# Start addresses of the activation tiles between two chained matrix products

## The chip, the cores and the metric

The kernel runs on one core of a Trainium2 chip. The metric is the device time of one execution in microseconds; less is better. The figure for the kernel before is the median of three runs.

## The reference

Attention with a causal mask over 2 batches, 12 heads, 448 positions and a head width of 64 gives 896 tokens of 768 features. Two MLPs follow, one on the other's output, each with a hidden width of 2048:

```
attn = softmax(scale * q @ k.T, causal) @ v          # [2, 12, 448, 64]
x = attn.transpose(0, 2, 1, 3).reshape(896, 768)
h = np.maximum(x @ w_in, 0.0);  x = h * h @ w_out    # first MLP
h = x @ w_in;  out = (h - np.tanh(h)) @ w_out        # second MLP
```

All is float32. The MLPs are 4 products of 896 x 768 x 2048.

## The kernel before

**Pieces.** To keep float32 accuracy, every operand of the MLPs is held as a high and a low part of type fp32r, one tile with both. A product of two such operands is three matmuls (`pieces`, lines 426 to 428): high weights by high activations, high weights by low activations, low weights by high activations. The weights are the stationary operand (128 x 128, one weight load for each matmul), the activations the moving one (128 x 448: one batch of tokens).

**Stages.** After attention (with the first groups of the first MLP woven in) come four halves: two MLPs, each with its hidden width in two halves. A half has an h stage and an o stage, of 288 matmuls each. In the h stage, `first` runs 16 groups of 18 matmuls (6 blocks of x, for 8 hidden blocks m and 2 batches b), and `act1` or `act2` makes an activation of each result, whose two parts are written by `hi_of` (ScalarE, line 436) and `lo_of` (VectorE, line 439). In the o stage, `second` runs 12 groups of 24 matmuls (8 hidden blocks k, for 6 output blocks m and 2 batches b) over these activations. Its results are added to `part`, become the next MLP's input (the x tiles again, then named y), or are written out. The order of instructions on each engine is that of the code, written out by hand.

**Tiles.** The input lies in 6 tiles x0 to x5 (y for the second MLP). The weights lie in a ring of 8 tiles w, filled from raw by three VectorE and two ScalarE instructions for each unit (`w_prep`). The activations g lie in 8 slots. A slot's tile is [P, 2, 2, S]: high or low, two hidden blocks, 448 tokens. `gdst` gives hidden blocks 2j and 2j + 1 of batch b the slot (5, 6, 0, 1, 3, 2, 4, 7)[4 b + j]. So in an o group of batch 0 blocks 0 to 3 come from slots 5 and 6, and 4 to 7 from slots 0 and 1. In a group of batch 1 blocks 0, 1 come from slot 3, blocks 2, 3 from slot 2, blocks 4, 5 from slot 4, blocks 6, 7 from slot 7. The same slots serve attention first: slots 0 to 2 hold the probabilities p, 3 and 4 their transposes pt, 7 the last rows of v (vend).

**Addresses.** Tiles lie one after another in each partition in the order in which the code first names them. Start addresses in bytes, modulo 256, as the built program has them: x (and y) 160; the ring w 96; slots 0, 1, 2 and 7 at 192; slots 3 to 6 at 96. The sizes of x, w and g tiles, of one block of 448 values and of one 128-column block of weights are all multiples of 256 bytes. So every x lies 64 bytes above its weights modulo 256, every g of slots 3 to 6 lies 0 above, and every g of slots 0, 1, 2 and 7 lies 96 above. Modulo 1024, each of these classes takes several values: both operands change with batch, part and block.

Of the kernel before, what the change touches and what calls it, by code (L numbers as in the profile page):

```python
# [9 lines left out]
F32R = mybir.dt.float32r  # L10
# [9 lines left out]
B, H, S, D = 2, 12, 448, 64  # L20
DM = H * D
DFF = 2048
P = 128
# [4 lines left out]
NPAIR = B * NP  # L28
NQ = S // D
RING = 8  # L30
UNIT = 6
UC = UNIT * P
NU = 2 * (KF + DFF * DM // (P * UC))
# [50 lines left out]
def body(ctx: ExitStack, tc: tile.TileContext, qT, kT, vL, w1, w2, w3, w4, out):  # L84
# [9 lines left out]
    def slot(i, shape, dt, name):  # L94
        return sb.tile(shape, dt, tag=f"slot{i}", name=name)
# [72 lines left out]
    def ring(u):  # L168
        taken.append(u)
        return sb.tile([P, 2, UC], F32R, tag="w", bufs=RING, name=f"w{u}")  # L170

    def room():
        i = len(taken) - RING
        return i < 0 or taken[i] < freed[0]
# [85 lines left out]
    def hbank(name):  # L260
        n = hcount[0] % 8
        hcount[0] += 1
        tag, bufs = ("s", 4) if n < 4 else ("t", 2) if n < 6 else ("oh"[n - 6], 1)
        return ps.tile([P, 512], F32, tag=tag, bufs=bufs, name=name)[:, :S]
# [152 lines left out]
    g = {}  # L417
# [13 lines left out]
    def group(*args):  # L431
        for _ in pieces(*args):
            pass
# [58 lines left out]
    gt = {}  # L492

    def gdst(l, half, m, b):

        if m % 2 == 0:
            i = (5, 6, 0, 1, 3, 2, 4, 7)[4 * b + m // 2]
            gt[b, m // 2] = slot(i, [P, 2, 2, S], F32R, f"g{l}_{half}_{b}_{m // 2}")
        t = gt[b, m // 2]
        g[m, b] = (t[:, 0, m % 2], t[:, 1, m % 2])  # L500
        return g[m, b]
# [5 lines left out]
    def first(l, half, m, b):  # L507

        u = (2 * l + half) * 2 * HALF + m
        dst = gdst(l, half, m, b)  # L510
        h = hbank(f"h{u}_{b}")
        for _ in first_pieces(l, half, m, b, h):
            pass
        if b == 1:
            freed[0] = u + 1
        return lambda: (act1, act2)[l](h, dst)


    def early(count):
        for m in range(count):  # L520
            dst = gdst(0, 0, m, 0)
            h = ps.tile([P, 512], F32, tag="h", bufs=1, name=f"h{m}_0")[:, :S]
            for k, _ in enumerate(first_pieces(0, 0, m, 0, h)):
                if k == KD - 1:
                    done.append((h, dst))
                yield
# [28 lines left out]
    def second(l, half, m, b):  # L555
        u0 = (2 * l + half) * 2 * HALF + HALF
        o = hbank(f"o{u0}_{m}_{b}")
        group(o, lambda k: (u0 + (m * HALF + k) // UNIT, (m * HALF + k) % UNIT), HALF, lambda k: g[k, b])
        if b == 1:
            freed[0] = u0 + (m + 1) * HALF // UNIT  # L560
        if half == 0:
# [26 lines left out]
    for s in range(NPAIR + 2):  # L588
        p, a = s - 1, s - 2
        ss, sp, sa = s < NPAIR, 0 <= p < NPAIR, a >= 0  # L590
        f = s - 2 >= NP
# [158 lines left out]
```

## Time and profile before

| what | before |
|---|---|
| median of 3 runs | 546.22 us (546.01 to 546.26) |
| the profiled execution's own time | 546.67 us |
| its span, first to last instruction | 544.9 us |
| TensorE matmul busy / weight load busy | 538.6 us / 483.6 us |
| VectorE / ScalarE / GpSimd busy | 346.5 us / 327.7 us / 3.2 us |
| MLP matmuls in h stages / in o stages | 1152 / 1152 |

The four o stages start 132.88, 249.33, 365.78 and 482.23 us after the span's start, the h stages of the second to fourth half 191.72, 308.17 and 424.61 us after it. Busy time of matmuls is from issue to a modelled end, and overlaps the next one. How fast TensorE goes is read from the distance of one start to the next, called the pitch here.

### The profile page before, as it was taken

To read this page: it belongs to the slowest core of one execution; us is meant where nothing else is said; L and a number is where in the kernel's file an instruction comes from. 1 tells how busy PE (TensorE), PEld (TensorE's weight loads), DVE (VectorE), ACT (ScalarE), POOL (GpSimd) and SP (SyncE) were. 2 spreads that over 40 slices of the span, in tenths; PEclk is the share of its full clock that TensorE was granted. 3 is DMA by queue.
4 is the path that set the end of the run, shared out by engine and by line. 5 is a ranking of instruction groups with operands and counts; after the bars stand their busy time and mean duration, and the time that the engine had idled before them with its cause. 6 is when DMAs were issued, how large, how long until landed. Compare 5 with 4: busy or idle time off the path is not lost.

```text
span 544.9 us, 8255 instructions
## 1 busy us (share of the span) xinstructions
PE 538.6 (99%) x3206; PEld 483.6 (89%) x3206; DVE 346.5 (64%) x730; ACT 327.7 (60%) x630; POOL 3.2 (1%) x21
## 2 busy tenths in 40 slices
PE   8999999999999999999999999999999999999997
PEld 5777878899999999999999999999999999999996
DVE  5998997664525155543554688988653588887301
ACT  6999996677424276664332388876543688854100
POOL 1000000000000000000000000000000000000000
PEclk9999999999999999999999999999999999999999
DMA  8862323352524243331333230113655301026111
GB/s 297 282 202 64 114 89 98 112 187 99 184 109 140 92 124 109 115 117 58 117 115 117 64 112 0 59 58 119 228 179 170 117 1 58 1 75 220 39 52 51
DMA packets 16022, 61.86 MB, mean 114 GB/s; under 512 B 1712, under 2 KB 7344, under 8 KB 15984
## 3 DMA queue, kind: packets, MB, share of 16 engines
q1 hardware_dynamic: 15696, 61.00, 33.6%
q8 instruction: 25, 0.41, 0.3%
q10 hardware_dynamic: 288, 0.34, 0.2%
q14 instruction: 13, 0.11, 0.1%
HBM read 58.59 MB, written 2.75 MB: 113 GB/s over the span
## 4 chain that ended last, share of the span: by engine, by line
PE 94%; DVE 3%; ACT 2%; issue 0%; DVEq 0%; POOLq 0%; ACTq 0%
PE h L426 14%; PE o L428 14%; PE o L427 14%; PE o L426 14%; PE h L428 14%; PE h L427 14%; PE o L378 3%; PE s L298 2%; PE t L366 2%; DVE p L313 1%; ACT p L331 1%; ACT pt L373 1%; DVE p L352 1%; PE warm L244 1%; DVE x L414 0%
## 5 line engine op out<-in xcount | busy, mean ns | idle before, releaser
L428 PE MATMUL o<-g,w 128*128 128x448 f32 x384 | 140.9, 367 | 0.0
L427 PE MATMUL o<-g,w 128*128 128x448 f32 x384 | 140.7, 366 | 0.0
L426 PE MATMUL o<-g,w 128*128 128x448 f32 x384 | 140.6, 366 | 0.0
L427 PEld LDWEIGHTS o<-g,w 128*128 128x128 f32 x384 | 72.1, 188 | 6.4
L428 PEld LDWEIGHTS o<-g,w 128*128 128x128 f32 x384 | 72.1, 188 | 6.4
L426 PEld LDWEIGHTS o<-g,w 128*128 128x128 f32 x384 | 72.1, 188 | 6.2
L426 PE MATMUL h<-x,w 128*128 128x448 f32 x192 | 71.3, 371 | 0.0
L426 PE MATMUL h<-y,w 128*128 128x448 f32 x192 | 69.7, 363 | 0.0
L428 PE MATMUL h<-x,w 128*128 128x448 f32 x192 | 69.7, 363 | 0.0
L428 PE MATMUL h<-y,w 128*128 128x448 f32 x192 | 69.6, 362 | 0.0
L427 PE MATMUL h<-x,w 128*128 128x448 f32 x192 | 69.4, 362 | 0.0
L427 PE MATMUL h<-y,w 128*128 128x448 f32 x192 | 69.1, 360 | 0.0
L137 DVE SCALAR_TENSOR_TENSOR raw<-raw 128x768 int32<-128x768 int32 x64 | 61.0, 954 | 12.1 <-ACT raw L123 12.1
L140 ACT CAST w<-raw 128x768 fp32r<-128x768 f32 x56 | 50.3, 899 | 26.9 <-DVE raw L137 26.9
L123 ACT ACTIVATE raw<-raw 128x768 f32<-128x768 f32 x64 | 58.9, 920 | 0.1
L153 DVE TENSOR_TENSOR w<-raw,w 128x768 fp32r<-128x768 f32 x32 | 30.6, 958 | 34.9 <-ACT w L140 34.8
L566 ACT COPY part<-o 128x448 f32<-128x448 f32 x24 | 12.8, 534 | 57.9 <-PE o L428 57.9
L151 DVE SCALAR_TENSOR_TENSOR w<-w,raw 128x768 fp32r<-128x768 f32 x32 | 30.6, 957 | 24.3 <-ACT w L140 24.2
L439 DVE TENSOR_TENSOR g<-r,g 128x448 fp32r<-128x448 f32 x32 | 20.0, 624 | 41.0 <-ACT g L436 41.0
L331 ACT ACTIVATE p<-p,st 128x320 f32<-128x320 f32 (+6 forms) x84 | 41.0, 516 | 4.0 <-DVE st L313 3.9
L428 PEld LDWEIGHTS h<-y,w 128*128 128x128 f32 x192 | 36.0, 188 | 2.9
L428 PEld LDWEIGHTS h<-x,w 128*128 128x128 f32 x192 | 36.1, 188 | 2.5
(57 smaller groups left out, 726.1 us busy)
## 6 DMA issues: line engine op xcount, KB each, us to landing
raw<-w SPq DMA_DIRECT2D x64, 768.0 KB, 4.2
q<-qT SPq DMA_DIRECT2D x12, 224.0 KB, 5.4
k<-kT SPq DMA_DIRECT2D x11, 224.0 KB, 3.8
out<-part SPq DMA_DIRECT2D x11, 224.0 KB, 1.9
v<-vL SPq DMA_DIRECT2D x2, 576.0 KB, 7.4
v<-vL SPq DMA_DIRECT2D x1, 1152.0 KB, 6.0
k<-kT ACTq DMA_DIRECT2D x1, 224.0 KB, 3.5
vend<-vL SPq DMA_DIRECT2D x2, 96.0 KB, 7.3
```

Of the source, the lines that this page charges most:

```text
L123: nc.scalar.activation(h, h, AF.Prelu, scale=2.0**-112, alpha=2.0**32)
L137: nc.vector.scalar_tensor_tensor(out=lo, in0=hi, scalar=3, in1=lo, op0=ALU.logical_shift_left, op1=ALU.bitwise_or)
L140: act_late.append(lambda: nc.scalar.copy(out=st["w"][:, 0], in_=lo.bitcast(F32)))
L151: nc.vector.scalar_tensor_tensor(out=w[:, 1], in0=w[:, 0].bitcast(F32), scalar=-(1.0 - 2.0**-24), in1=f, op0=ALU.mult, op1=ALU.add)
L153: nc.vector.tensor_sub(out=w[:, 1], in0=f, in1=w[:, 0])
L331: nc.scalar.activation(p, p, AF.Exp, bias=st[:, 0, i : i + 1], scale=-1.0, **kw)
L378: return nc.tensor.matmul(ob[n][D * j : D * j + D, o], lhsT=vs[b][kc][rows, D * h : D * h + D], rhs=rhs, skip_group_check=True, **flags).ins
L426: nc.tensor.matmul(h, lhsT=hi, rhs=xh, start=(k == 0), stop=False)
L427: nc.tensor.matmul(h, lhsT=hi, rhs=xl, start=False, stop=False)
L428: nc.tensor.matmul(h, lhsT=lo, rhs=xh, start=False, stop=(k == kk - 1))
L439: nc.vector.tensor_sub(out=dst[1], in0=v, in1=dst[0])
L566: nc.scalar.copy(out=part[m][:, b], in_=o)
```

## The change

Each slot's tile becomes 64 floats (256 bytes) longer, and g is a view into it that starts 56 floats (224 bytes) into slots 0, 1, 2 and 7, and 16 floats (64 bytes) into slots 3 to 6. With 192 + 224 = 416 and 96 + 64 = 160, every g then starts at 160 modulo 256, as x does. The tiles p, pt and vend of attention still start at their slot's begin. A slot takes 256 bytes more, so all that lies behind it moves by a multiple of 256: w by 1536 bytes against x (six slots lie ahead of it), the slots by 0 to 1792.

```diff
+LINE = 64
+G_AT = (56, 56, 56, 16, 16, 16, 16, 56)
...
         if m % 2 == 0:
             i = (5, 6, 0, 1, 3, 2, 4, 7)[4 * b + m // 2]
-            gt[b, m // 2] = slot(i, [P, 2, 2, S], F32R, f"g{l}_{half}_{b}_{m // 2}")
+            n = 2 * 2 * S
+            t = slot(i, [P, n + LINE], F32R, f"g{l}_{half}_{b}_{m // 2}")
+            gt[b, m // 2] = t[:, G_AT[i] : G_AT[i] + n].rearrange("p (z k s) -> p z k s", z=2, k=2)
         t = gt[b, m // 2]
```

## Rows read from the trace of the kernel before

**Rows 1.** Page, parts 1 and 2: busy time; granted TensorE clock by slices, in tenths.
```profile
PE 538.6 (99%) x3206; PEld 483.6 (89%) x3206; DVE 346.5 (64%) x730; ACT 327.7 (60%) x630; POOL 3.2 (1%) x21
...
PEclk9999999999999999999999999999999999999999
```
**Rows 2.** Page, part 4: chain that ended last, by engine.
```profile
PE 94%; DVE 3%; ACT 2%; issue 0%; DVEq 0%; POOLq 0%; ACTq 0%
```
**Rows 3.** Weight loads by line: count, busy us, mean ns, idle us before them.
```profile
L427 PEld LDWEIGHTS o<-g,w 128*128 128x128 f32 x384 | 72.1, 188 | 6.4
L426 PEld LDWEIGHTS o<-g,w 128*128 128x128 f32 x384 | 72.1, 188 | 6.2
L428 PEld LDWEIGHTS o<-g,w 128*128 128x128 f32 x384 | 72.1, 188 | 6.4
...
L428 PEld LDWEIGHTS h<-y,w 128*128 128x128 f32 x192 | 36.0, 188 | 2.9
...
L426 PEld LDWEIGHTS h<-y,w 128*128 128x128 f32 x192 | 36.0, 188 | 1.9
...
L427 PEld LDWEIGHTS h<-y,w 128*128 128x128 f32 x192 | 35.9, 187 | 2.5
```
**Rows 4.** Timeline of TensorE, last half: start us, duration us; stages' ends.
```profile
424.61 0.36 PE L426 MATMUL h<-y,w 128*128 128x448 f32 x1
...
482.23 0.36 PE L426 MATMUL o<-g,w 128*128 128x448 f32 x1
...
540.86 0.37 PE L428 MATMUL o<-g,w 128*128 128x448 f32 x1
```
**Rows 5.** Timeline of TensorE: two o groups, each slot's first matmul.
```profile
487.12 0.36 PE L426 MATMUL o<-g,w 128*128 128x448 f32 x1
...
488.33 0.37 PE L426 MATMUL o<-g,w 128*128 128x448 f32 x1
...
489.57 0.37 PE L426 MATMUL o<-g,w 128*128 128x448 f32 x1
...
490.79 0.37 PE L426 MATMUL o<-g,w 128*128 128x448 f32 x1
...
492.03 0.37 PE L426 MATMUL o<-g,w 128*128 128x448 f32 x1
...
494.46 0.37 PE L426 MATMUL o<-g,w 128*128 128x448 f32 x1
...
496.93 0.36 PE L426 MATMUL o<-g,w 128*128 128x448 f32 x1
```
**Rows 6.** Windows, last h and o stage: length, busy by engine (count), clock, DMA.
```profile
424.60:482.10 57.50, 57.50 (x289) 53.88 (x288) 48.92 (x83) 46.72 (x83) 0.00 (x0) 1.00 0.16 55
482.20:541.20 59.00, 59.00 (x289) 53.89 (x288) 24.52 (x36) 12.88 (x17) 0.00 (x0) 1.00 0.24 83
```
**Rows 7.** Timeline, all engines, at the last o stage's beginning.
```profile
485.51 0.61 DVE L439 TENSOR_TENSOR g<-w,g 128x448 fp32r<-128x448 f32 x1
...
486.50 0.37 PE L426 MATMUL o<-g,w 128*128 128x448 f32 x1
...
490.32 0.96 DVE L153 TENSOR_TENSOR w<-raw,w 128x768 fp32r<-128x768 f32 x1 [0.49 <-ACT w L140]
```
**Rows 8.** Low parts, line 439: count, duration ns min, median, max.
```profile
L439 DVE TENSOR_TENSOR g<-w,g x32: 612/616/627, 319.9 to 487.3; 128x448 fp32r<-128x448 f32 x32
L439 DVE TENSOR_TENSOR y<-part,y x12: 617/619/627, 255.8 to 309.8; 128x448 fp32r<-128x448 f32 x12
```
**Rows 9.** Weight loads of attention that read slots, or whose matmuls do.
```profile
L366 PEld LDWEIGHTS t<-ident,p 128*128 128x128 f32 x168 | 18.9, 141 | 3.0 <-ACT pt L373 0.6 <-issue 0.4 <-DVE p L352 0.3
...
L378 PEld LDWEIGHTS o<-pt,v 128*64 128x64 f32 x144 | 9.4, 136 | 9.7 <-issue 3.5 <-ACT pt L373 3.3 <-DVE st L313 0.3
L378 PEld LDWEIGHTS o<-pt,v 64*64 64x64 f32 x144 | 6.2, 133 | 2.1 <-issue 1.2 <-ACT p L331 0.3 <-ACT r L547 0.3
L378 PEld LDWEIGHTS o<-pt,vend 64*64 64x64 f32 x48 | 3.7, 132 | 0.4 <-POOL token L402 0.4
```

## The prediction

> **What bounds the kernel now.** I read the page first. [...] The chain of waits lies on PE for 94% [rows 2], so a nanosecond taken off a matmul counts unless a wait fills it. A busy share of 99% does not say that the matmuls go as fast as they can, since their ends are modelled and overlap. So I went on to the weight loads by line, where idle time between loads shows [rows 3], then to the starts in the timeline [rows 4 and 5], then to a table of two stages [rows 6], and last to the producers with least time in hand [rows 7].
>
> The weight loads are all 188 ns long, but those of o stages have more idle time before them. The o rows sum to 3 x 72.1 busy and 6.4 + 6.2 + 6.4 idle, 235.3 us for 1152, or 204.3 ns each. The h rows with y sum to 107.9 + 7.3 = 115.2 us for 576, or 200.0 ns each [rows 3]. The starts say the same: 424.61 to 482.23 us is 288 pitches of 200.1 ns (taken within each stage of the last three halves, unrounded, 200.04), and 482.23 to 540.86 us is 287 pitches of 204.3 ns [rows 4]. All four o stages have 204.3.
>
> The instructions of both are the same in shape. Is it then the operands' addresses? Within an o stage the pitch goes by the slot that is read. In the group of batch 1 from 487.12, slots 3 and 4 take 1.21 and 1.22 us for 6 matmuls, slots 2 and 7 take 1.24 and 1.24. In the group of batch 0 from 492.03, slots 5 and 6 take 2.43 us for 12 matmuls (202.5 ns), slots 0 and 1 take 2.47 (205.8) [rows 5]. These are two of 48 groups. Over all 48, from the same timeline, slots 5 and 6 have 203.0, slots 3 and 4 202.9, slots 0 and 1 205.4, slots 2 and 7 205.8. So g that stands 0 above its weights modulo 256 costs 203, g that stands 96 above costs 205.6, and x, 64 above, costs 200.0. The same two slot classes recur in both batches at other places of the group, so the place in the group doesn't make it. Nor does other engines' traffic: the last h stage, with VectorE busy 48.92 us and ScalarE 46.72, is the faster one; the last o stage has 24.52 and 12.88 [rows 6].
>
> **The change part by part.** No instruction is added or removed, no queue's order changes, no wait is added.
>
> *The o matmuls.* Every g comes to x's residue, 160, while w stays at 96. The pairs then stand 64 apart, and x's pairs take all four values that this allows modulo 1024 and run at one pitch. I take x's pitch: 1152 x (204.29 - 200.04) = 4.90 us less. Bounds: nothing, if addresses don't act; as the most, the smallest pitch that recurs in the trace, 197 to 198 ns (one of three matmuls in every h block, followed by two of 201), 1152 x 7 = 8 us; that one is part of a triple whose mean is 200, so I keep 200.0.
>
> *Writers and readers of g.* ScalarE's and VectorE's writes start at another offset. Low parts written to y, whose tiles have the new residue already, take 619 ns at the median, to g 616 [rows 8]: 3 ns longer each, under 0.1 us for 16 in an h stage, on an engine that isn't the bound there. I cost it at nothing; a longer write would first show where the least time is in hand (below).
>
> *Attention.* p, pt, vend and one v tile move by multiples of 256, so their residues modulo 256 stay. Whether a longer period counts there no row shows. The loads concerned sum to 38.2 busy and 15.2 idle, 53.4 us [rows 9]. If they changed by what separates the two slot classes, 2.6 of 204 ns or 1.3%, that is 0.7 us either way. I take 0.
>
> *The h stages.* x's residues and w's stay modulo 256: 0. w moves 1536 bytes against x; that is a rival below.
>
> *What is late next.* A faster o stage brings each use nearer to its producer. The tightest is the last g of batch 0 in the second MLP: its low part ends 485.51 + 0.61 = 486.12, and its first matmul, the 22nd of the o stage, starts 486.50 [rows 7]. 0.38 us in hand; 21 x 4.25 ns take 0.09 of it and leave 0.29. Next is a weight unit: VectorE ends 491.28 [rows 7], the matmul starts 494.46 [rows 5], 60 matmuls into the stage, so 3.18 goes to 2.92. These producers start from the h results before them, so gains of earlier stages move both sides alike. Nothing stalls. Behind the last matmul, 540.86, stands a tail of some 4 us to the span's end that the change doesn't touch.
>
> *The sum.* 546.67 (the profiled execution) - 4.90 = 541.77. That execution lies 0.45 us above the median, 546.22, so for a median: 546.22 - 4.90 = 541.3 us, 0.9% less.
>
> [...] The rows above show the pitch going with the slot, 203 to 205.6, at the same weights [rows 5]. [...]
>
> **The rivals.**
>
> 1. *Only part of it is the distance.* Modulo 64 a distance of 64 is the same as 0, which slots 3 to 6 have already. If that were the rule, those 576 matmuls would gain nothing, the other 576 would fall from 205.6 to 203.0, 1.5 us: 544.7. For it: the two classes within o are the only contrast with all else equal; h differs from o also in group length and in the tiles its weights come from. Against it: the 200 of h would then need another cause, and the o pitch within slots 3 to 6 swings between 202 and 207 by block, which no x block does. Chance 0.09.
>
> 2. *Addresses don't act; the pitch goes by something that the slot number stands for*, such as the order of the blocks in the group. Then 0: 546.2. Against it: the classes recur at other places in batch 0 and batch 1. Chance 0.07.
>
> 3. *A longer period counts, and the ring's move spoils the h stages.* w goes 1536 bytes away from x. If the quiet pairing of x rested on a period above 1024, the h stages could take the o pitch, 1152 x 4.25 = 4.9 us more, and o, paired after another distance than x was, would gain nothing: 551.1. If only h lost it and o won it the two would cancel; so it decides the sign from the point where h loses more than o gains. Against it: x tiles lie 7168 bytes apart and ring tiles 6144, so pairs in h already stand at many distances, and every x block has one pitch. Chance 0.05.
>
> **How the numbers follow.** The forecast has 0.79, and its own range is 540.6 to 542.1: 0.7 us of attention either way, and the spread of medians. The range for 8 in 10 reaches to 540.2 at the low end (a part of the low bound) and to 543.4 at the high end, for a partial gain between forecast and first rival. About 0.2%, 1.1 us, is what a measurement of this kernel can tell from no change. Faster by more than that: 0.79 and most of the first rival, 0.07, is 0.86. Same: the second rival and the rest of the first, 0.09. Slower: the third, 0.05.
>
> **What would show it.** Right: idle time before o loads falls from 19.0 us to about 14.6; the o pitch is 200 in every slot, so an o stage takes 57.4 us from first to last start instead of 58.6, and the three later ones start about 1.2, 2.4 and 3.7 us earlier; h rows stay at 200.0; no idle at the 22nd matmul of an o stage. Wrong: slots 3 to 6 stay at 203 (first rival), all o pitches stay (second), h pitch rises above 200 (third), or transposes and value products change their pitch, which would show attention's bound to count.

## The result, and the profile after

The changed kernel takes 541.26 us (median of 4 runs, 540.96 to 541.73), the kernel before beside it 546.24 us (546.01 to 546.61): ratio 0.9908, 95% interval 0.9896 to 0.9920. The forecast was 541.3 us, range 540.2 to 543.4.

The profiled execution of the changed kernel took 541.23 us, its span 539.4 us. Lines 31 to 497 of the code have moved by two, so 426 to 428 are now 428 to 430. The weight loads by line (count, busy us, mean ns, idle us before), against [rows 3]:

```profile
L428 PEld LDWEIGHTS o<-g,w 128*128 128x128 f32 x384 | 72.1, 188 | 5.6
L429 PEld LDWEIGHTS o<-g,w 128*128 128x128 f32 x384 | 72.1, 188 | 3.7
L430 PEld LDWEIGHTS o<-g,w 128*128 128x128 f32 x384 | 71.8, 187 | 5.1
...
L428 PEld LDWEIGHTS h<-y,w 128*128 128x128 f32 x192 | 36.0, 188 | 2.7
L429 PEld LDWEIGHTS h<-y,w 128*128 128x128 f32 x192 | 36.0, 188 | 2.0
...
L430 PEld LDWEIGHTS h<-y,w 128*128 128x128 f32 x192 | 35.9, 187 | 2.6
```

The loads are as long as before. The idle time before o loads is 14.4 us in place of 19.0 (14.6 was forecast); h is as it was. In the timeline of TensorE (start us, duration us), the last half's stage ends, against [rows 4]:

```profile
420.46 0.36 PE L428 MATMUL h<-y,w 128*128 128x448 f32 x1
...
478.06 0.36 PE L428 MATMUL o<-g,w 128*128 128x448 f32 x1
...
535.46 0.36 PE L430 MATMUL o<-g,w 128*128 128x448 f32 x1
```

h: 57.60 us over 288 pitches, 200.0 ns. o: 57.40 over 287, 200.0 ns, where it was 204.3. From these and the rows of before, the saving at successive places is 4.15 us at the last h stage's start, 4.17 at the last o stage's, 5.40 at the last matmul. Three o stages lie ahead of the first two places and the fourth behind them, so the last o stage brings 1.23, and four of them 4.9. Another 0.4 us is there before the first o stage begins (132.46 us against 132.88). Nothing ties that part to the change: in the ten experiments below whose x and w keep their distance, this start lies anywhere from 132.12 to 132.90 us. The medians, 4.98 us apart, hold the o stages' 4.9 and next to nothing else.

By slot, against [rows 5], the first o groups of batch 1 and batch 0 in the last stage:

```profile
482.86 0.36 PE L428 MATMUL o<-g,w 128*128 128x448 f32 x1
...
484.06 0.36 PE L428 MATMUL o<-g,w 128*128 128x448 f32 x1
...
485.26 0.36 PE L428 MATMUL o<-g,w 128*128 128x448 f32 x1
...
486.46 0.36 PE L428 MATMUL o<-g,w 128*128 128x448 f32 x1
...
487.66 0.36 PE L428 MATMUL o<-g,w 128*128 128x448 f32 x1
...
490.06 0.36 PE L428 MATMUL o<-g,w 128*128 128x448 f32 x1
...
492.46 0.36 PE L428 MATMUL o<-g,w 128*128 128x448 f32 x1
```

1.20 us for 6 matmuls and 2.40 for 12, in every slot. The producers with least time in hand, against [rows 7], in the timeline of all engines:

```profile
481.34 0.61 DVE L441 TENSOR_TENSOR g<-w,g 128x448 fp32r<-128x448 f32 x1
...
482.26 0.36 PE L428 MATMUL o<-g,w 128*128 128x448 f32 x1
...
486.18 0.96 DVE L155 TENSOR_TENSOR w<-raw,w 128x768 fp32r<-128x768 f32 x1 [0.51 <-ACT w L142]
```

The last g ends at 481.95 and is used at 482.26: 0.31 us in hand (0.29 forecast). The weight unit ends at 487.14 and is used at 490.06 (the row above): 2.92, as forecast.

### The profile page after: what moved, and what is told of

The parts are those of the page before. It is cut to its first block, busy times and chain, and to the rows that moved or that the text cites. A ratio compares the mean times of both kernels' runs of the same rounds, so it can differ in the third digit from the quotient of the medians.

```text
span 539.4 us, 8255 instructions
## 1 busy us (share of the span) xinstructions
PE 532.9 (99%) x3206; PEld 482.7 (89%) x3206; DVE 346.2 (64%) x730; ACT 327.5 (61%) x630; POOL 3.2 (1%) x21
## 4 chain that ended last, share of the span: by engine, by line
PE 93%; ACT 3%; DVE 3%; DMA 1%; issue 0%; DVEq 0%; POOLq 0%; ACTq 0%
PE h L428 15%; PE o L429 14%; PE h L429 14%; PE o L428 14%; PE h L430 14%; PE o L430 14%; PE o L380 3%; PE s L300 2%; PE t L368 2%; ACT p L333 2%; DVE p L315 1%; ACT pt L375 1%; DVE p L354 1%; DMA k<-kT 1%; DVE x L416 0%; DVE w L155 0%
## 5 line engine op out<-in xcount | busy, mean ns | idle before, releaser
L429 PE MATMUL o<-g,w 128*128 128x448 f32 x384 | 139.4, 363 | 0.0
L428 PE MATMUL o<-g,w 128*128 128x448 f32 x384 | 139.2, 362 | 0.0
L430 PE MATMUL o<-g,w 128*128 128x448 f32 x384 | 138.2, 360 | 0.0
L134 DVE TENSOR_SCALAR raw<-raw 128x768 int32<-128x768 int32 x64 | 35.5, 555 | 7.1 <-DMA raw<-w 7.1
```

The lines of the kernel that those rows point to most:

```text
L134: nc.vector.tensor_scalar(out=lo, in0=lo, scalar1=29, scalar2=None, op0=ALU.logical_shift_right)
L428: nc.tensor.matmul(h, lhsT=hi, rhs=xh, start=(k == 0), stop=False)
L429: nc.tensor.matmul(h, lhsT=hi, rhs=xl, start=False, stop=False)
L430: nc.tensor.matmul(h, lhsT=lo, rhs=xh, start=False, stop=(k == kk - 1))
```

## The experiments

A pitch below is the mean time from one matmul's start to the next in one trace, over a whole stage or over a slot's 24 blocks of six matmuls. Where one stage holds one distance for 288 matmuls, its slots agree within half a ns (at distance 56 within 0.8). "Distance" is start of g (or x) less start of w, in bytes modulo 256. "Against" sets a time beside that of the kernel before, measured alongside.

**1. Only the room.**

```diff
-G_AT = (56, 56, 56, 16, 16, 16, 16, 56)
+G_AT = (0, 0, 0, 0, 0, 0, 0, 0)
```

> The slots keep their 256 extra bytes, but every g starts at its slot's begin again. Distance theory (the start distance of g to its weights modulo 256 sets the pitch, 64 giving 200 ns): distances 0 and 96 return, o pitch 204.3 ns, 546.2 us, the gain is gone whole. Rival, the room: the longer slots, which move the weight ring by 1536 bytes and the slots by 256 to 1792, make the gain; then the o pitch stays 200.0 and the time 541.3 us.

Measured 545.96 us against 546.37, ratio 0.9997 (0.9988 to 1.0006). The idle before o loads is back:

```profile
L429 PEld LDWEIGHTS o<-g,w 128*128 128x128 f32 x384 | 72.1, 188 | 6.5
L428 PEld LDWEIGHTS o<-g,w 128*128 128x128 f32 x384 | 72.1, 188 | 6.3
L430 PEld LDWEIGHTS o<-g,w 128*128 128x128 f32 x384 | 72.1, 188 | 6.4
```

19.2 us against 19.0 before. The o pitch is 204.3 and h stays at 200.04, though the ring and the slots have moved by their multiples of 256. So the start of g inside its slot makes the whole gain, and the rival of the room falls.

**2. Offsets for four slots.**

```diff
-G_AT = (56, 56, 56, 16, 16, 16, 16, 56)
+G_AT = (56, 56, 56, 0, 0, 0, 0, 56)
```

> Only slots 0, 1, 2 and 7 get their offset (distance 64); slots 3 to 6 stay at distance 0. Distance theory: slots 0, 1, 2, 7 at 200.0 ns, slots 3 to 6 at about 203.0, o mean 201.5; 576 x 3.0 ns = 1.7 us above the changed kernel, 543.0 us. Rival, uniformity: what counts is that all pairs have one and the same distance, so that a mix of two costs in every slot; then slots 0, 1, 2, 7 stay above 202 ns too and the time is 544.5 us or more.

Measured 545.06 us against 546.37, ratio 0.9976 (0.9966 to 0.9985): 2 us more than the distance theory said. The timeline of TensorE, a group of batch 1 and one of batch 0:

```profile
486.01 0.37 PE L428 MATMUL o<-g,w 128*128 128x448 f32 x1
...
487.25 0.36 PE L428 MATMUL o<-g,w 128*128 128x448 f32 x1
...
488.45 0.37 PE L428 MATMUL o<-g,w 128*128 128x448 f32 x1
...
490.89 0.37 PE L428 MATMUL o<-g,w 128*128 128x448 f32 x1
...
493.37 0.36 PE L428 MATMUL o<-g,w 128*128 128x448 f32 x1
...
495.77 0.37 PE L428 MATMUL o<-g,w 128*128 128x448 f32 x1
```

Slot 2 (distance 64) takes 1.20 us for 6, and slots 0 and 1 take 2.40 for 12: 200 ns, beside neighbours of another distance. Uniformity falls. But slot 3 takes 1.24, and slots 5 and 6 take 2.48 for 12: 206.7 ns at distance 0, where the same slots had 203 in the kernel before and in experiment 1. Only their neighbours' distance had changed, from 96 to 64. A matmul's pitch is not set by its own distance alone. Nor is it only the matmuls next to a change of distance that differ: slot 6, the seventh to twelfth matmul in a row at distance 0, has 202.3 on average in the kernel before and 206.7 here.

**3 and 4. A distance of its own for each slot**, in steps of 32 bytes, and the steps between.

```diff
-G_AT = (56, 56, 56, 16, 16, 16, 16, 56)
+G_AT = (40, 48, 56, 24, 32, 40, 48, 32)    # 3
+G_AT = (44, 52, 60, 28, 36, 44, 52, 36)    # 4
```

> Each slot gets a distance of its own to the weights modulo 256: slots 0 to 7 at 0, 32, 64, 96, 128, 160, 192, 224 bytes. Distance theory: slot 0, formerly 96 and now 0, goes to about 203 ns; slot 2 (64) has 200.0; slot 3, formerly 0 and now 96, goes to about 205.6; h stages stay at 200.0; the others show the curve, expected between 200 and 208. Rival, the slot's place (its number, or its place in the group): the pitch stays with the slot, slots 0 and 3 do not swap their classes. Rival, uniformity: all eight slots at 203 or more.

> The same at the distances between: slots 0 to 7 at 16, 48, 80, 112, 144, 176, 208, 240 bytes. Distance theory: a smooth curve between the values of the even map, with a flat stretch of 200 ns near 64 if 64 is no isolated point. A distance below 200.0 ns anywhere would point to a faster version. Rival, the slot's place: the same slots as in the other map are slow, whatever their distance.

Pitches of slots 0 to 7: 205.1, 204.5, 200.3, 205.2, 201.8, 206.2, 202.2, 204.5 in the even map; 202.0, 202.8, 203.2, 204.0, 205.0, 204.2, 203.8, 202.4 in the odd one (one trace each; 545.76 and 545.49 us). Slot 2, now at 64 by itself, is within 0.3 ns of the 200.0 of x (205.8 before), so the rival of the slot's place falls. Slots 0 and 3 did not swap 205.6 for 203 as the distance theory expected; both stand at 205. In slot 0 at distance 16 the six pitches of a block average 205, 207, 200, 200, 200, 200: the pitch changes within a block, and these maps mix the distance with what came before.

**5, 6 and 7. One distance for all slots.**

```diff
-G_AT = (56, 56, 56, 16, 16, 16, 16, 56)
+G_AT = (40, 40, 40, 0, 0, 0, 0, 40)      # 5: distance 0
+G_AT = (0, 0, 0, 24, 24, 24, 24, 0)      # 6: 96
+G_AT = (8, 8, 8, 32, 32, 32, 32, 8)      # 7: 128
```

> Every g at distance 0 from its weights modulo 256. Theory of the prediction (a matmul's pitch goes by its own distance alone: 0 gives 203, 96 gives 205.6, 64 gives 200): o pitch 203.0 ns, 541.3 + 1152 x 3.0 ns = 544.7 us. Theory of the carried state (after the run with four offsets, where slots 3 to 6 ran at 206.8 ns beside neighbours at 64, but at 203 beside neighbours at 96): the pitch also goes by the distance of the matmuls before, and with one distance throughout it settles at 206.8 ns, with one and the same triple of pitches in every block; 541.3 + 1152 x 6.8 ns = 549.1 us. Theory of uniformity (any single distance does): 200 ns, 541.3 us.

> Every g at distance 96. Own distance alone: o pitch 205.6 ns, 547.7 us. Carried state: a settled value between 200 and 209 ns, the same triple in every block, not tied to 205.6; 541.3 to 551.7 us. Uniformity: 200 ns, 541.3 us.

> Every g at distance 128, half of the period. Own distance alone: the 201.8 ns that slot 4 had at 128 in the even map, 543.3 us. Carried state: a settled triple, any value from 200 ns up. If 200.0 ns is a floor that other things set, nothing lies below it; a pitch under 200 would make a faster kernel than the changed one.

Measured 549.02 us against 546.18 (ratio 1.0051, 1.0035 to 1.0068) at 0, 547.25 (1.0023, 1.0013 to 1.0032) at 96, 545.73 in one run at 128. The weight loads of o, in this order of kernels:

```profile
L429 PEld LDWEIGHTS o<-g,w 128*128 128x128 f32 x384 | 72.1, 188 | 7.2
L428 PEld LDWEIGHTS o<-g,w 128*128 128x128 f32 x384 | 72.1, 188 | 7.2
L430 PEld LDWEIGHTS o<-g,w 128*128 128x128 f32 x384 | 72.1, 188 | 7.4
```
```profile
L430 PEld LDWEIGHTS o<-g,w 128*128 128x128 f32 x384 | 72.1, 188 | 6.7
L428 PEld LDWEIGHTS o<-g,w 128*128 128x128 f32 x384 | 72.1, 188 | 6.7
L429 PEld LDWEIGHTS o<-g,w 128*128 128x128 f32 x384 | 72.1, 188 | 6.8
```
```profile
L429 PEld LDWEIGHTS o<-g,w 128*128 128x128 f32 x384 | 72.1, 188 | 6.2
L428 PEld LDWEIGHTS o<-g,w 128*128 128x128 f32 x384 | 72.1, 188 | 6.2
L430 PEld LDWEIGHTS o<-g,w 128*128 128x128 f32 x384 | 72.1, 188 | 6.2
```

The starts give 206.67, 205.3 and 204.0 ns. At distance 0, 541.26 + 1152 x 6.67 ns = 548.9 us, and 549.02 was measured: own distance alone (544.7) and uniformity (541.3) are out. The kernel before mixed 0 and 96 in halves and had 204.29, less than either has when alone, whose mean is 206.0. All of that came to the slots at 0: they had 203.0 there and have 206.67 alone, while those at 96 had 205.4 to 205.9 there and have 205.3 alone. A constant triple, which the expectations looked for, is there only at 0 (every pitch within 205 to 208 ns). At 96 and 128 the single pitches keep cycling, from 197 to 210 and from 195 to 213 ns, and 205.3 and 204.0 are their means.

**8. The ring moved against x.** The ring goes 32 bytes further, and so does g.

```diff
-G_AT = (56, 56, 56, 16, 16, 16, 16, 56)
+G_AT = (64, 64, 64, 16, 16, 16, 16, 64)
...
-    token = sb.tile([P, 1], F32, name="token")
+    token = sb.tile([P, 9], F32, name="token")[:, :1]
```

> The weight ring (with what lies behind token) moves by 32 bytes, to 128 modulo 256, and every g by 32, to 192; x stays at 160. So o keeps distance 64 at other addresses, and h goes to distance 32. If the distance counts: o stays at 200.0 ns, h leaves 200 and settles at one triple of its own. If the activations' own residue counts (160, that of x): h stays at 200.0, o leaves it. If the weights' residue counts (96): both leave it.

Measured 547.95 us against 546.18, ratio 1.0031 (1.0018 to 1.0044). The weight loads:

```profile
L428 PEld LDWEIGHTS o<-g,w 128*128 128x128 f32 x384 | 72.1, 188 | 3.9
L430 PEld LDWEIGHTS o<-g,w 128*128 128x128 f32 x384 | 72.1, 188 | 5.6
L429 PEld LDWEIGHTS o<-g,w 128*128 128x128 f32 x384 | 71.8, 187 | 5.0
L429 PEld LDWEIGHTS h<-y,w 128*128 128x128 f32 x192 | 36.1, 188 | 3.5
L428 PEld LDWEIGHTS h<-y,w 128*128 128x128 f32 x192 | 36.1, 188 | 3.6
L430 PEld LDWEIGHTS h<-y,w 128*128 128x128 f32 x192 | 36.1, 188 | 3.5
```

o keeps 14.5 us of idle, 200.0 ns, at other addresses of both operands. h, with x where it was, goes to 10.6 us (7.3 before) and 206.67 ns. Of the three cases in the expectation only the first fits: it is the distance of the two operands that counts, not where either lies (tried with this one shift of both). And what the o stages won, the h stages can lose.

**9, 10 and 11. A distance for each o stage.** Each stage holds one distance for 288 matmuls. The edit is shown against the changed kernel.

```diff
-G_AT = (56, 56, 56, 16, 16, 16, 16, 56)
+G_BASE = (96, 96, 96, 0, 0, 0, 0, 96)
+DIST = (16, 48, 80, 112)      # 10: (160, 192, 224, 240); 11: (56, 60, 68, 72)
...
+            at = (DIST[2 * l + half] - G_BASE[i]) // 4 % LINE
...
-            gt[b, m // 2] = t[:, G_AT[i] : G_AT[i] + n].rearrange("p (z k s) -> p z k s", z=2, k=2)
+            gt[b, m // 2] = t[:, at : at + n].rearrange("p (z k s) -> p z k s", z=2, k=2)
```

> One distance for all slots of an o stage, another for each of the four o stages: 16, 48, 80, 112 bytes. With one distance for 288 matmuls each stage settles. Carried state and distance: four different pitches between 200.0 and 207 ns, each constant through its stage; between 0 and 32 (both 206.67) 16 could be 206.67 too, although slot 0 fell to 200 at 16 in the odd map. If 64 is an isolated point, 48 and 80 stand above 204; if it lies in a window, one of them is at 200.0.

> The same with 160, 192, 224, 240 bytes. If the magnitude of the distance counts and not its sign, 192 (64 below the weights) has 200.0 as 64 has, 224 has the 206.67 of 32, 160 the 205.3 of 96. If the sign counts, these differ. If 200.0 ns is a floor, no stage is below it.

> The same with 56, 60, 68, 72 bytes, 4 and 8 bytes around 64. If 64 is a window of some width, 60 and 68 have 200.0 ns; if steps of the memory's own line count, the four split at 64 with a jump; if 64 is a sharp point, all four stand above 203.

The three took 546.07, 545.20 and 546.04 us, one run each, against 545.99. The timeline of TensorE in the last of the three (its lines are one further): first matmul of the second o stage (distance 60), of the h stage after it, of the third o stage (68), of the h stage after that.

```profile
248.52 0.36 PE L429 MATMUL o<-g,w 128*128 128x448 f32 x1
...
306.22 0.36 PE L429 MATMUL h<-y,w 128*128 128x448 f32 x1
...
363.84 0.37 PE L429 MATMUL o<-g,w 128*128 128x448 f32 x1
...
423.36 0.36 PE L429 MATMUL h<-y,w 128*128 128x448 f32 x1
```

57.70 us at 60 and 59.52 us at 68: 200.4 and 206.7 ns, 8 bytes apart. In the second of the three, the first matmul of the o stage at 192 and of the h stage after it:

```profile
249.24 0.37 PE L429 MATMUL o<-g,w 128*128 128x448 f32 x1
...
307.49 0.37 PE L429 MATMUL h<-y,w 128*128 128x448 f32 x1
```

58.25 us, 202.3 ns. The pitches of stages that hold one distance, one trace each:

| distance | ns | distance | ns | distance | ns |
|---|---|---|---|---|---|
| 0 | 206.67 | 60 | 200.4 | 112 | 206.7 |
| 16 | 202.2 | 64 | 200.0 | 128 | 204.0 |
| 32 | 206.67 | 68 | 206.7 | 160 | 206.7 |
| 48 | 202.9 | 72 | 206.6 | 192 | 202.3 |
| 56 | 202.7 | 80 | 203.3 | 224 | 203.3 |
|  |  | 96 | 205.3 | 240 | 202.7 |

The sign counts (192, which is 64 below, has 202.3), and 128 bytes more make a difference (0 and 128, 64 and 192). 64 is neither an isolated point nor inside a window: among steps of 4 bytes it is the last before an edge. None of these 17 means is below 200.0, so no faster version showed; the other 47 steps of 4 bytes were not tried. The o stages at the other distances were entered from an h stage at 64 (the h stages at 32 from o stages at 64). Since slot 6 of the kernel before had 202.3 at distance 0 up to the twelfth matmul in a row, a distance need not have one pitch alone, and the table has the one reached from 64.

**12. Low weights at another distance.**

```diff
-        return sb.tile([P, 2, UC], F32R, tag="w", bufs=RING, name=f"w{u}")
+        return sb.tile([P, 2, UC + 32], F32R, tag="w", bufs=RING, name=f"w{u}")[:, :, :UC]
```

> The low weights of each ring tile start 128 bytes (modulo 256) further than the high ones, so they stand at distance 192 from their activations and the high ones at 64, in h and o alike. If the weight load that runs beside a matmul counts (the load of the next one's weights), the pitch that changes is that after the second matmul of a triple, beside which the low weights are loaded. If a matmul's own weights count, it is the pitch after the third. If 192 is as good as 64, nothing changes: 200.0 ns in both stages.

Measured 551.24 us in one run against 545.99. Both stages have 204.45 ns, and the three pitches of a triple are 204, 206 and 203 where the changed kernel has about 201, 201 and 198. The weight loads of o:

```profile
L428 PEld LDWEIGHTS o<-g,w 128*128 128x128 f32 x384 | 72.6, 189 | 6.8
L430 PEld LDWEIGHTS o<-g,w 128*128 128x128 f32 x384 | 72.2, 188 | 6.6
L429 PEld LDWEIGHTS o<-g,w 128*128 128x128 f32 x384 | 71.8, 187 | 5.5
```

Idle time rose before all three, by 1.2, 1.5 and 1.8 us (3 to 5 ns each). The expectation looked for one pitch that changes, and all three did, so the run doesn't tell the load beside a matmul from a matmul's own weights. It does show that mixing 64 with 192 (200.0 and 202.3 when alone) costs more than either.

## Why the prediction was right, point by point

*The bound.* TensorE's issue from start to start, with nothing waiting: right. 4.9 of the 4.98 us came from the pitch, and the two producers near their limit moved as worked out (0.31 and 2.92 us left).

*The sum.* 1152 x (204.29 - 200.04) was 4.90; the traces have 204.29 to 200.01, 4.93. It stood on two means of whole stages, and on the choice of x's pitch for g. No row said how wide the good place is (4 bytes further the pitch is 206.7); copying x's distance to the byte made that harmless. Experiment 1 shows that the start of g is what did it; experiment 8 that the distance, not the place, is what g took over from x.

*The low bound.* The 197 to 198 ns were taken for part of a triple with mean 200. The changed kernel bears that out: its o triples have about 201, 201 and 198, 200.0 on average. It was not the smallest pitch that recurs: in the kernel before, slot 3's first matmul has 195 to 196 ns in 23 of its 24 groups, followed by 199 and 207, so that one is no bound for a whole stage either.

*What was wrong in it.* "So g that stands 0 above its weights modulo 256 costs 203, g that stands 96 above costs 205.6." Alone, 0 costs 206.67 and 96 costs 205.3: the order is the reverse. The 205.6 was near; the 203 was what 0 costs behind matmuls at 96. The contrast between slots within a stage pointed to addresses, rightly, and its direction meant nothing, since each slot's matmuls ran in a state left by those before. The sum used no class's figure, so it wasn't touched. The expectation for experiment 2 used 203, and missed by 2 us. Of slots 3 to 6 the prediction says that the pitch swings between 202 and 207 by block; by blocks of three matmuls it is 200.3 to 206.0. And the first x block of the last three h stages had 204, all others 200 (in the changed kernel, behind o stages at 64, that block has 200 too): one more trace of what came before.

*The first rival* (64 is as good as 0 modulo 64): out, slots 3 to 6 went from 203 to 200, and 0 settles at the dear end. *The second* (addresses don't act): out by experiments 1 and 8. In this stream of loads and matmuls the operands' addresses alone make up to 6.7 ns of 200 (h in experiment 8: 200.0 to 206.67); by what mechanism, no run shows. *The third* (a period above 1024 spoils h): out, h has 200.01 after the ring's 1536 bytes. Its mechanism in small, a ring that moves against x, is experiment 8, and there h did lose 6.7 ns a matmul.

*Attention* was costed at 0. Its loads have the idle times of [rows 9] again to a tenth (3.0, 9.7, 2.1 and 0.4 us). *The writers of g* were costed at 0 too, and the low parts of [rows 8] still take 616 ns at the median.

*What stays open.* Why 64 is good and 68 is not; by what the state is carried from one matmul to the next; and whether the weights that count are a matmul's own or those loaded beside it (in the trace of before the next matmul's load starts 2 to 4 ns after a matmul's start). Experiment 12 was to show the last and didn't.

## What to carry to other kernels

In a stream of weight loads and matmuls that waits for nothing, compare the start-to-start pitch of stages with the same shapes (here 200.0 in h against 204.3 ns in o); where they differ, compare the operands' start addresses, here modulo 256 (in experiment 1, moves by multiples of 256 left 200.04 and 204.3 as they were). Copy a distance that a whole stage of the same kernel already runs at its best pitch, with all operands at that one distance, and check after any change of tile sizes: in experiment 8, 32 bytes ahead of the ring cost this kernel 6.7 us, more than the 4.98 it had won. A contrast between tiles that alternate shows that something acts, not how much each would cost alone (here 203.0 beside 205.4 to 205.9 in the mix, 206.67 and 205.3 alone).

## What the runs showed of the hardware that was not expected

- At a granted clock of 0.998 to 1.0 of full speed in the profiled executions, the pitches of a 128 x 448 matmul of type fp32r with its own weight load, as means of stages at one distance, lie between 200.0 and 206.7 ns. Six of the 17 distances stand at the upper end.
- 4 bytes can make the whole of it: 200.0 at 64, 206.7 at 68.
- The pitch has a memory that outlasts six matmuls: at distance 0, the seventh to twelfth matmul in a row have 202.3 after 96 and 206.7 after 64. Distances 0 and 96 have 206.67 and 205.3 alone, 204.29 when they alternate; 64 and 192 have 200.0 and 202.3 alone, 204.45 when each triple has two at 64 and one at 192.
